# Gated delta-rule attention with a softplus feed-forward: the layout of the transposed inverses, and where the key norm is applied

## The chip, the cores and the metric

The kernel runs on one core of a Trainium2 chip, in one launch. The metric is device time in microseconds (us), median of the runs. A core has a matrix engine (PE in the profile; loading its stationary operand is listed apart, as PEld), a vector engine (DVE), an activation engine (ACT), a general engine (POOL) and a queue engine (SP) that here only starts DMAs. Each engine works through its own instruction stream in order; semaphores tie the streams together.

## The reference

```
k_n = k / (norm(k) + 1e-6)
for t in range(768):                      # for each of 4 batches x 8 heads
    readout = q[t] @ state                # state: 48 x 48
    y[t]    = g[t] * readout
    state  += beta[t] * outer(k_n[t], v[t] - state^T k_n[t])
x   = y laid out as (3072 tokens, 384)
out = softplus(x @ w_in) @ w_out          # 384 -> 2048 -> 384
```

All inputs and the output are float32; the kernel calculates in float16 with float32 accumulation.

## The kernel before

The recurrence is cut into 12 chunks of 64 steps. Inside a chunk it is solved in closed form: with the Gram matrix of the chunk's keys, a 64x64 unit triangular system per head has to be inverted. Each 64x64 inverse is built from 32x32 blocks, and each of these from 16x16 blocks. Between chunks only the state is passed on. The feed-forward ("dense") part of a chunk, or of a pair of chunks, can start once that chunk's y is there, and it fills the matrix engine while the recurrence of later chunks waits.

Work is described as items, each with the engines that may run it. One hand-laid string, `_ORDER`, lists all items with engine letters (D, A, G = POOL, P, S); it sets the order of every engine's stream, and buffers are given out in that order too.

The items by stage, with their lines:

- **front** (L262): the k and q of a chunk are cast to float16 ("cast", L200 on POOL or DVE, L198 on ACT), transposed on PE (L289), copied out ("kev"), and multiplied into the Gram matrices (L396, L397). The keys are raw here, not divided by their norm. "kkc" copies the negated key Gram blocks to `kk`; "mask" (L414) the masked query Gram blocks to `mt`.
- **norms** (L435), for a pair of chunks: square (ACT, L441), reduce (DVE, L445), root (on ACT at L456 for the first two pairs, else as a power of one half on POOL, L461), plus 1e-6 (L464). "lbeta" (L472) transposes the norms, takes the reciprocal, and multiplies it twice into beta: four short DVE instructions.
- **inverse** (L467), for a pair of chunks: "ln" (L481) transposes 32x32 blocks of `kk` on DVE; 15 substitution steps of two instructions each (L504, L511) invert the 16x16 diagonal blocks, on DVE for the first pair, on POOL for the other five; "c16" casts the result to `tw`. Then DVE transposes it back: "tn" once (L524) and "t32" twice (L534), in 32x32 blocks. Two PE products (xmm L555, tmm L576 and L582), with the copies "xs" and "td2" behind them, complete the 32x32 inverses in `td`; zmm (L608, L611) and its copy make `z`, the off-diagonal part.
- **chain** (L632), chunk after chunk: "vs" (L657) multiplies v by the norm, on POOL or DVE; ks and qs multiply with the state (L649); w = v - ks (L681); umm (L690, L694) applies the 32x32 inverses, zu (L715) the rest; smm and "s" update the state (L735, L750); ymm and "y" give the output (L765, L780); ytr transposes it (L797).
- **dense** (L812): g1 (L825), softplus on ACT (L837), g2 (L852), copy and store.

The layout that the change is about: `tn` is `[P, U, 16]` and `td` is `[P, U, HC]`, with U = 32 the blocks and HC = 32 the columns. A block's columns lie side by side for PE. The DVE transposes write them through a rearranged view:

```python
tn.ap.rearrange("p u j -> p j u")                        # L525: step of 16 elements
td.ap.rearrange("p u i -> p i u")[:, 16*b : 16*b + 16]   # L535: step of 32 elements
```

PE reads them as moving columns, `tn.ap[r, u, :]` and `td.ap[QUAD[qd], u, 16:]`, and in umm as the stationary operand, `td.ap[f, 16*cl + 2*pi + m, :]`.

Of the kernel before, what the change touches and what calls it, by code (L numbers as in the profile page):

```python
# [11 lines left out]
F16 = mybir.dt.float16  # L12
AF = mybir.ActivationFunctionType
ALU = mybir.AluOpType

# [59 lines left out]
def kernel(  # L75
# [11 lines left out]
    nc = tc.nc  # L87
# [54 lines left out]
    r_tn = ring("tn", 2, [P, U, 16], F16)  # L142
    r_xs = ring("xs", 2, [P, U, 16], F16)
    r_td = ring("td", 3, [P, U, HC], F16)
# [6 lines left out]
    r_ga = ring("ga", 18, [P, 512], F16)  # L151
# [33 lines left out]
    for t in r_t16.tiles:  # L185
        nc.vector.memset(t, 0.0)
    for t in r_kqt.tiles:
        nc.vector.memset(t[:, 4 * NP * C :], 0.0)
# [73 lines left out]
    def front(c, kk):  # L262
# [5 lines left out]
        for name, ring_ in (("k", r_kn), ("q", r_qn)):  # L268
# [3 lines left out]
            for h in range(parts):  # L272
                sl = slice(h, h + 1) if parts == 2 else slice(0, 2)
                x_it.append(
# [160 lines left out]
    def norms(cs, nv, on_act):  # L435
# [17 lines left out]
        tag = f"{cs[0]}"  # L453
        if on_act:
            root = add("sqrt", tag, "A",
                       lambda en: nc.scalar.activation(nv.ap, nv.ap, AF.Sqrt),  # L456
                       deps=red, bufs=[nv])
            root_last[0] = root
        else:
            root = add("pow", tag, "G",  # L460
                       lambda en: nc.gpsimd.tensor_tensor(nv.ap, nv.ap, half_c, ALU.pow),  # L461
                       deps=red, bufs=[nv])
        return add("eps", tag, "D",
                   lambda en: nc.vector.tensor_scalar_add(nv.ap, nv.ap, 1e-6),  # L464
                   deps=[root], bufs=[nv])

    def inverse(cc, kk, kk_it, nv, nv_it):  # L467
        tag = f"{2 * cc}"
        first = cc == 0
        nl, bl = Buf(r_nl), Buf(r_bl)  # L470

        def lbeta(en):  # L472
            nc.vector.transpose(nl.ap, nv.ap)
            nc.vector.reciprocal(nl.ap, nl.ap)
            nc.vector.tensor_tensor(bl.ap, beta_l[:, cc], nl.ap, ALU.mult)
            nc.vector.tensor_tensor(bl.ap, bl.ap, nl.ap, ALU.mult)

        bl_it = add("lbeta", tag, "D", lbeta, deps=[nv_it], bufs=[nv, nl, bl])
# [11 lines left out]
                       bl.ap.rearrange("p (b i) -> p b i", b=2),  # L490
                   ),
                   deps=[prev, bl_it], bufs=[tt, bl])

        def prep(en, b):
            r = slice(16 * b, 16 * b + 16)
            eng.tensor_tensor(  # L496
                nn.ap[:, b], ln.ap[:, r, r], bl.ap[:, r, None].broadcast_to([P, 16, 16]),
                ALU.mult,
            )
# [13 lines left out]
        for b in range(2):  # L513
            prev = add("prep", f"{tag}.{b}", en0, lambda en, b=b: prep(en, b),
                       deps=[l1, prev, bl_it], bufs=[ln, nn, bl])
        for j in range(15):
# [8 lines left out]
                        tn.ap.rearrange("p u j -> p j u"),  # L525
# [4 lines left out]
        for b in range(2):  # L530

            def t32(en, b=b):
                c0 = 16 - 16 * b
                nc.vector.transpose(  # L534
                    td.ap.rearrange("p u i -> p i u")[:, 16 * b : 16 * b + 16],  # L535
# [10 lines left out]
        halves = [[0], [1]] if first else [[0, 1]]  # L546
        td2 = {}
        e3s = []
        for cl in range(2):

            def xmm(en, cl=cl):
                for u in range(16 * cl, 16 * cl + 16):
                    for qd in range(4):
                        r = slice(32 * qd, 32 * qd + 16)
                        nc.tensor.matmul(  # L555
                            uv(xp.ap)[QUAD[qd], u], kk.ap[r, 0, u, :], tn.ap[r, u, :]
                        )

            e3s.append(add("xmm", f"{2 * cc + cl}", "P", xmm, deps=[tn_it], bufs=[kk, tn, xp],
# [9 lines left out]
        e5s = []  # L569
        for cl in range(2):  # L570

            def tmm(en, cl=cl):
                us = slice(16 * cl, 16 * cl + 16)
                for qd in range(4):
                    r = QUAD[qd]
                    nc.tensor.matmul(  # L576
                        uv(ep.ap)[r, us], ident[r, r], td.ap[r, us, 16:],
                        start=True, stop=False, skip_group_check=True,
                    )
                for u in range(16 * cl, 16 * cl + 16):  # L580
                    for qd in range(4):
                        nc.tensor.matmul(  # L582
                            uv(ep.ap)[32 * qd : 32 * qd + 16, u],
                            xs.ap[QUAD[qd], u, :],
                            td.ap[QUAD[qd], u, 16:],
# [5 lines left out]
            e5s.append(add("tmm", f"{2 * cc + cl}", "P", tmm, deps=[e4s[cl]] + td_its,  # L591
                           bufs=[xs, td, ep], mm=68, mode="3232"))
        for hs in halves:
            us = slice(16 * hs[0], 16 * hs[-1] + 16)
            it = add("td2", f"{2 * cc + hs[0]}", "AD",
                     lambda en, us=us: copy(en, td.ap[:, us, 16:], uv(ep.ap)[:, us]),
# [392 lines left out]
```

## Time and profile before

| | |
|---|---|
| runs | 308.46, 310.68, 305.07 us; median 308.46 |
| the profiled execution | 306.28 us |
| its span in the profile | 304.6 us |
| mean granted PE clock in the span | 0.943 |
| ACT busy | 131.4 us |
| POOL busy | 120.5 us |
| DMA moved | 27.69 MB in 107704 packets |
| code fetches on the instruction queue q8 | 47 packets, 0.77 MB |

The span is what the profile shows from the program's first instruction to its last; the execution's own time has another 1.7 us around it. An engine's busy time counts overlapping instructions once. The page's slices cut the span into 40 parts of 7.6 us; a digit is the busy tenths of a slice. A group line names the source line, engine, operation, the tiles written and read, the shapes and the count; behind the first bar are the busy time and the mean duration of one, behind the second the idle time of that engine just before them and what ended it. The view of waits lists who waited for whom, with the total, the number of times and the longest.

### The profile page before, as it was taken

The numbers are of one execution on the slowest core, as the hardware profiler recorded it, in microseconds if no ns is written. First come the engines' busy times: TensorE is split into PE (matmuls) and PEld (weight loads), VectorE is DVE, ScalarE is ACT, GpSimd is POOL, SyncE is SP. The second block draws the span as 40 slices with busy tenths as digits, with TensorE's granted clock in tenths as the row PEclk, the third lists the DMA queues.
The fourth block names the chain that finished last, engine by engine and source line by source line (L and its number), as shares of the span: only waits on it lengthen the run. The fifth ranks groups of instructions, "written<-read, shape, count | busy, mean of one in ns | idle before, by whom it ended". The sixth has DMA issues, their size and how long they took to land.

```text
span 304.6 us, 13469 instructions
## 1 busy us (share of the span) xinstructions
PE 241.7 (79%) x6112; PEld 160.8 (53%) x6112; DVE 184.7 (61%) x348; ACT 131.4 (43%) x250; POOL 120.5 (40%) x219
## 2 busy tenths in 40 slices
PE   1432347789959996869877999969899969999993
PEld 1232236568637763446643565635566635577771
DVE  7789936367696776974873467668486193432100
ACT  4541413347513666244423466613553425433441
POOL 7205335008892588458516203885007810000000
PEclk9999999999969999799985799995999988999999
DMA  9999999999900197983979521341035110002113
GB/s 126 152 140 151 171 143 181 185 168 142 130 2 4 31 163 130 156 132 55 167 109 146 109 56 30 62 68 30 4 83 106 27 28 18 14 22 63 26 26 78
DMA packets 107704, 27.69 MB, mean 91 GB/s; under 512 B 100864, under 2 KB 107648, under 8 KB 107648
## 3 DMA queue, kind: packets, MB, share of 16 engines
q1 hardware_dynamic: 101600, 23.21, 48.5%
q0 software_dynamic: 3968, 3.25, 6.7%
q8 instruction: 47, 0.77, 1.1%
q10 hardware_dynamic: 2080, 0.39, 0.9%
q14 instruction: 9, 0.07, 0.1%
HBM read 25.26 MB, written 4.72 MB: 98 GB/s over the span
## 4 chain that ended last, share of the span: by engine, by line
PE 46%; DVE 21%; POOL 17%; issue 10%; ACT 3%; DMA 2%; DVEq 0%; POOLq 0%; ACTq 0%
PE h L825 14%; PE o L852 14%; POOL tmp L504 8%; POOL tt L511 7%; DVE td L534 4%; DVE tn L524 3%; DVE ln L481 3%; PE d L649 3%; DMA kf<-in_k_dram 2%; PE d L715 2%; DVE tt L511 2%; PE d L289 2%; POOL nn L496 2%; DVE tmp L504 2%; PE d L765 1%
## 5 line engine op out<-in xcount | busy, mean ns | idle before, releaser
L825 PE MATMUL h<-xt,w_in 128*128 128x512 f16 (+1 forms) x384 | 82.0, 352 | 0.0
L852 PE MATMUL o<-w_out,ga 128*128 128x384 f16 x384 | 77.7, 345 | 2.3 <-issue 1.7
L837 ACT ACTIVATE ga<-h 128x512 f16<-128x512 f32 x96 | 56.3, 596 | 40.3 <-PE h L825 33.6
L852 PEld LDWEIGHTS <-ga 128*128 128x128 f16 x384 | 37.3, 102 | 28.9 <-issue 8.9
L825 PEld LDWEIGHTS <-w_in 128*128 128x128 f16 x384 | 36.5, 103 | 22.6 <-issue 5.3
L504 POOL TENSOR_TENSOR tmp<-nn,tt 128x30 f32<-128x30 f32 (+7 forms) x75 | 29.0, 387 | 5.9
L511 POOL TENSOR_TENSOR tt<-tt,tmp 128x30 f32<-128x30 f32 (+7 forms) x75 | 27.7, 369 | 5.9
L534 DVE STREAM_TRANSPOSE td<-tw 128x512 f16<-128x512 f16 x12 | 28.7, 2452 | 0.0
L461 POOL TENSOR_TENSOR nv<-nv,half_c 128x32 f32<-128x32 f32 x4 | 21.8, 5446 | 9.1 <-DVE nv L445 9.1
L200 DVE CAST u<-d 128x384 f16<-128x384 f32 x23 | 12.5, 552 | 19.4 <-PE d L715 15.3
L414 DVE TENSOR_TENSOR mt<-d,mask 128x256 f16<-128x256 f32 x40 | 16.8, 435 | 9.8 <-ACT kk L198 6.7
L198 ACT ACTIVATE u<-d 128x384 f16<-128x384 f32 x25 | 12.1, 492 | 23.4 <-PE d L715 12.7
L198 ACT ACTIVATE kqt<-d 128x512 f16<-128x512 f16 x26 | 15.1, 597 | 16.0 <-PE d L289 10.4
L555 PE MATMUL d<-tn,kk 16*32 16x16 f16 x768 | 7.3, 173 | 16.8 <-DVE tn L524 13.3
L289 PE MATMUL d<-ident,kn 128*128 128x128 f16 x96 | 9.1, 250 | 13.1 <-DVE kn L200 6.1
L198 ACT ACTIVATE osb<-o 128x384 f32<-128x384 f32 x14 | 6.9, 492 | 27.2 <-PE o L852 26.9
L496 POOL TENSOR_TENSOR nn<-ln,bl 128x256 f32<-128x256 f16 x10 | 6.3, 650 | 30.9 <-DVE ln L481 30.9
L649 PE MATMUL d<-s,kqt 48*64 48x48 f16 x704 | 16.7, 192 | 1.7 <-issue 1.4
L649 PEld LDWEIGHTS <-kqt 48*64 48x64 f16 x704 | 13.5, 112 | 8.4 <-issue 7.7
L555 PEld LDWEIGHTS <-kk 16*32 16x32 f16 x768 | 7.1, 93 | 18.8 <-issue 15.2
L657 POOL TENSOR_TENSOR vf<-vf,nv 128x768 f32<-128x768 f32 x8 | 11.8, 1472 | 13.2 <-DMA vf<-in_v_dram 13.2
L780 DVE TENSOR_TENSOR yg<-d,gf 128x384 f16<-128x384 f32 x24 | 12.8, 551 | 5.7 <-PE d L765 5.6
(100 smaller groups left out, 405.1 us busy)
## 6 DMA issues: line engine op xcount, KB each, us to landing
qf<-in_q_dram SPq DMA_DIRECT2D x24, 192.0 KB, 5.7
vf<-in_v_dram SPq DMA_DIRECT2D x24, 192.0 KB, 5.8
gf<-in_g_dram SPq DMA_DIRECT2D x24, 192.0 KB, 5.5
out_dram<-osb SPq DMA_DIRECT2D x48, 96.0 KB, 2.2
kf<-in_k_dram SPq DMA_DIRECT2D x22, 192.0 KB, 5.5
w_in<-in_moe_w_in_dram POOLq DMA_DIRECT2D x4, 384.0 KB, 6.6
w_out<-in_moe_w_out_dram POOLq DMA_DIRECT2D x4, 384.0 KB, 10.2
kf<-in_k_dram ACTq DMA_DIRECT2D x2, 192.0 KB, 4.5
```

Source lines behind the costliest of these rows:

```text
L198: nc.scalar.activation(o, x, AF.Copy, scale=float(sign))
L289: nc.tensor.transpose(o[:, p, i], x.ap[:, p, 2 * i : 2 * i + 2].rearrange("p h d -> p (h d)"), ident,)
L414: nc.vector.tensor_tensor(mt[c][m].ap[:, NP * p : NP * p + NP], gb[m].ap.rearrange("p (n b) -> p n b", n=NP)[:, :, C:], mask[:, None, :].b ...
L461: lambda en: nc.gpsimd.tensor_tensor(nv.ap, nv.ap, half_c, ALU.pow),
L504: eng.tensor_tensor(t, nn.ap[:, :, j + 1 :, j : j + 1].broadcast_to([P, 2, n, w]), tt.ap[:, :, j : j + 1, :w].broadcast_to([P, 2, n, w]), ...
L511: eng.tensor_tensor(rows, rows, t, ALU.add)
L534: nc.vector.transpose(td.ap.rearrange("p u i -> p i u")[:, 16 * b : 16 * b + 16], tw.ap[:, b, :, c0 : c0 + 32],)
L555: nc.tensor.matmul(uv(xp.ap)[QUAD[qd], u], kk.ap[r, 0, u, :], tn.ap[r, u, :])
L649: nc.tensor.matmul(hd(o.ap)[HALF[r], NP * p + i], kq_of(c, p)[FEAT[m], 2 * i + r, off : off + C], s0[r].ap[FEAT[m], NP * p + i], **start(p ...
L825: nc.tensor.matmul(hp.ap[:, n * b : n * b + n], w_in[:, j, f * P : (f + 1) * P], xt.ap[:, j, t0 : t0 + n], start=(j == 0), stop=(j == 2),)
L837: lambda en, hp=hp, o=gb: nc.scalar.activation(o.ap, hp.ap, AF.Softplus),
L852: nc.tensor.matmul(op.ap[:, :DM], b.ap[:, col + c0 : col + c0 + 128], w_out[:, f, :], start=(f == 0), stop=(f == NF - 1),)
```

## The change

1. `tn` becomes `[P, 16, U]` and `td` becomes `[P, HC, U]`: the order in which the DVE transposes produce their elements, so they write without a step. PE now reads a block's columns with a step of 32 elements (64 bytes): in xmm, tmm and zmm as moving operand, in umm as stationary operand. The identity products of tmm and zmm write PSUM with a step too; td2's copy has both sides without one. `td` gets four buffers in place of three; `ga` 17 in place of 18.
2. For all chunks from 2 on, the cast of k is replaced by a multiplication with the reciprocal norm ("unit"). With that the Gram blocks need no norm: "lbeta" and "vs" go for these chunks, and a reciprocal is added behind the 1e-6. The first pair stays as it was.
3. The root may run on ACT or POOL for pairs from chunk 4 on. In the new order the pair 4/5 has it on ACT, behind the Softplus table load.
4. At the start, `kk`'s first half (three buffers) and `nv` (three) are set by DVE.
5. The first pair's xs and td2 are no longer done in two halves.
6. `_ORDER` is written anew for all engines; the number of items goes from 1227 to 1210.

```diff
+GROUPS = [[c, c + 1] for c in range(0, 12, 2)]
...
-    r_tn = ring("tn", 2, [P, U, 16], F16)
+    r_tn = ring("tn", 2, [P, 16, U], F16)
...
-    r_td = ring("td", 3, [P, U, HC], F16)
+    r_td = ring("td", 4, [P, HC, U], F16)
...
-    r_ga = ring("ga", 18, [P, 512], F16)
+    r_ga = ring("ga", 17, [P, 512], F16)
...
+    for t in r_kk.tiles:
+        nc.vector.memset(t[:, 0], 0.0)
+    for t in r_nv.tiles:
+        nc.vector.memset(t, 1.0)
...
+                if name == "k" and nv is not None:
+
+                    def unit(en, f=f, x=x):
+                        ENG[en].tensor_tensor(
+                            x.ap[:, :, :, :D],
+                            f.ap,
+                            nv.ap[:, 16 * cl : 16 * cl + 16]
+                            .rearrange("p (a h) -> p a h", a=2)[:, :, :, None]
+                            .broadcast_to([P, 2, H, D]),
+                            ALU.mult,
+                        )
+
+                    x_it.append(
+                        add("unit", f"kn{c}.{h}", "GD", unit, deps=fl + [nv_it], bufs=[f, x, nv])
+                    )
+                    continue
...
+        def sqrt(en):
+            if en == "A":
+                nc.scalar.activation(nv.ap, nv.ap, AF.Sqrt)
+            else:
+                nc.gpsimd.tensor_tensor(nv.ap, nv.ap, half_c, ALU.pow)
+
+        root = add("sqrt", tag, "A" if on_act else "GA", sqrt, deps=red, bufs=[nv],
+                   size=0 if on_act else 1)
...
+        def eps(en):
+            nc.vector.tensor_scalar_add(nv.ap, nv.ap, 1e-6)
+            if inv:
+                nc.vector.reciprocal(nv.ap, nv.ap)
...
-                        tn.ap.rearrange("p u j -> p j u"),
+                        tn.ap,
...
-                    td.ap.rearrange("p u i -> p i u")[:, 16 * b : 16 * b + 16],
+                    td.ap[:, 16 * b : 16 * b + 16],
...
-        halves = [[0], [1]] if first else [[0, 1]]
+        halves = [[c % 2 for c in cs]]
...
-                            uv(xp.ap)[QUAD[qd], u], kk.ap[r, 0, u, :], tn.ap[r, u, :]
+                            uv(xp.ap)[QUAD[qd], u], kk.ap[r, 0, u, :], tn.ap[r, :, u]
...
-                        uv(ep.ap)[r, us], ident[r, r], td.ap[r, us, 16:],
+                        iu(ep.ap)[r, :, us], ident[r, r], td.ap[r, 16:, us],
...
-                            uv(ep.ap)[32 * qd : 32 * qd + 16, u],
+                            iu(ep.ap)[32 * qd : 32 * qd + 16, :, u],
                             xs.ap[QUAD[qd], u, :],
-                            td.ap[QUAD[qd], u, 16:],
+                            td.ap[QUAD[qd], 16:, u],
...
-                     lambda en, us=us: copy(en, td.ap[:, us, 16:], uv(ep.ap)[:, us]),
+                     lambda en, us=us: copy(en, td.ap[:, 16:, us], iu(ep.ap)[:, :, us]),
...
-                    nc.tensor.matmul(o[f], ident[f, f], td.ap[f, 16 * cl : 16 * cl + 16])
+                    nc.tensor.matmul(
+                        o[f].rearrange("p u i -> p i u"),
+                        ident[f, f],
+                        td.ap[f, :, 16 * cl : 16 * cl + 16],
+                    )
...
-                            td.ap[QUAD[2 * r + 1], 16 * cl + u, :],
+                            td.ap[QUAD[2 * r + 1], :, 16 * cl + u],
...
-        vs = add("vs", f"{c}", "GD",
+        vs = None if nv is None else add("vs", f"{c}", "GD",
...
-                            o[f, pi], td.ap[f, 16 * cl + 2 * pi + m, :], w1.ap[f, pi]
+                            o[f, pi], td.ap[f, :, 16 * cl + 2 * pi + m], w1.ap[f, pi]
...
-        nv_it = norms(cs, nv, cc < 2)
-        inverse(cc, kk, kk_it, nv, nv_it)
+        inv = cs[0] > 1
+        kk_it = []
+        nv_it = norms(cs, nv, cs[0] < 4, inv)
+        for c in cs:
+            kk_it += front(c, kk, nv if inv else None, nv_it)
+        inverse(cs, kk, kk_it, nv, nv_it, inv)
...
 _ORDER = """
-S8 A9 D126 D154 P129 D130 A1 A125 P127 A148 D149 P140 S0 G104 D142 A128 P137 D139 A146 A141 D147
...
+S8 A9 D131 P133 S0 A1 S11 S16 S2 S10 A132 A106 P135 S17 A136 D107 D134 S3 G111 A104 D154 G110 P114
...
```

In the new order POOL has all ten unit multiplications. Its stream around the first of them, with item names in place of numbers, runs: two parts of w_in, vs of chunk 1, unit of chunk 2, the other two parts of w_in, unit of chunk 3, the four parts of w_out, then the first POOL inverse; behind that inverse unit 5, unit 4, the root of pair 6, unit 6, unit 7, and the inverse of pair 4.

## The prediction

> **What bounds the kernel now.** I read the busy table and the slices first, then the chain of work that ended last, then the waits, then the groups of the transposes, then the chain in order of time around one stall.
>
> ```profile
> PE 241.7 (79%) x6112; PEld 160.8 (53%) x6112; DVE 184.7 (61%) x348; ACT 131.4 (43%) x250; POOL 120.5 (40%) x219
> PE   1432347789959996869877999969899969999993
> DVE  7789936367696776974873467668486193432100
> PEclk9999999999969999799985799995999988999999
> DMA  9999999999900197983979521341035110002113
> PE 46%; DVE 21%; POOL 17%; issue 10%; ACT 3%; DMA 2%; DVEq 0%; POOLq 0%; ACTq 0%
> ```
>
> PE is the engine to relieve: from slice 8 (about 61 us) on it is full except in a few dips. At the dips of slices 11, 16, 20, 27 and 32 DVE is busy, and the granted clock falls too. Ahead of 60 us PE is mostly idle, waiting for the first two chunks while DMA is full.
>
> ```profile
> PE d L555 <- DVE tn L524: 13.3, 5, 3.6
> PE d L576 <- DVE td L534: 2.5, 2, 2.2
> PE d L715 <- issue: 4.5, 2, 2.3
> L534 DVE STREAM_TRANSPOSE td<-tw 128x512 f16<-128x512 f16 x12 | 28.7, 2452 | 0.0
> L524 DVE STREAM_TRANSPOSE tn<-tw 128x512 f16<-128x512 f16 x6 | 14.3, 2377 | 2.6 <-POOL tw L200 2.4
> L481 DVE STREAM_TRANSPOSE ln<-kk 128x1024 f16<-128x1024 f16 x6 | 11.4, 1907 | 2.2 <-ACT kk L198 2.0
> ```
>
> The first row of waits is the largest that PE has: five of the six inverses end with PE standing for tn. The transposes explain it: ln moves 1024 elements per partition in 1907 ns, tn and td only 512 in 2377 and 2452. ln reads with a step and writes without; td reads without and writes with one. So the stepped write costs most of a td, and tn, which has both, is no slower.
>
> ```profile
> 83.98 0.47 DVE tw L200
> 84.48 2.37 DVE tn L524
> 86.89 1.19 PE d L555 x114
> 88.08 4.93 PE o L852 x16
> ...
> 263.88 2.60 PE o L852 x16
> ```
>
> One inverse ends: cast, tn, then xmm; PE stood 3.55 us (from 83.34). The 16 dense products after it take 4.93 us, at 264 us the same 16 take 2.60: the throttle granted half the clock. So a stall is paid twice.
>
> **The change part by part.** Sums are against the profiled execution, 306.28 us (span 304.6 and 1.7 around it); the median is 308.46, 2.2 higher, the three runs lie between 305.07 and 310.68.
>
> *Transposes on DVE.* No contiguous 16-bit transpose of this size is in the trace. Nearest: DVE copies from PSUM, 256 elements in 415 ns (L202) and 512 in 690 (z, L200): 1.07 ns an element and 141 fixed, so td comes to 141 + 512 x 1.07 = 690 ns. tn keeps a stepped read; by ln, 1907/1024 = 1.86 ns an element, 950 ns. Ends for td: no gain (2450), if the transpose itself is slow, which ln's 1.86 against 4.8 speaks against; 690 as the good end. I take 690: 12 x 1.76 = 21 us and 6 x 1.43 = 8.6 us less on DVE. Most lies beside PE's work. On the path: at the start tn and both t32 stand in line (tn from 27.5, second t32 ends 35.20): 1.43 + 2 x 1.7 = 4.9 us. In the five later groups tn's 1.43 each: 7.2. The PE wait for td in the pair 6/7: 2.2. Total 14.3. What is late next: c16, the PE-ACT-PE steps through xs and td2, and code fetches, which the rows call issue.
>
> *Clock.* The granted clock is 0.943 of the span: 304.6 x 0.057 = 17 us lost to the half clock, of which PE works some 15 (the half-speed stretches hold few idle us). Here the trace and a page of the Trainium skill differ. The stretches start shortly behind PE stalls of 3.55, 2.54, 2.19, 2.82 and 2.90 us (at 83, 120, 156, 203 and 245 us). The Trainium skill, "TensorE: Matmul & The Clock Gate", section "HAM oscillation — how this bites in real kernels", gives the rule as no idle gap above about 3.4 us. By the rule only the first stall would trip it, and shortening the others would bring nothing: 3.4 us (half of one stretch of about 7). By the trace gaps under 3 us do it too, beside the tiny xmm products, and shortening all could return 15. I take the middle, 7: gaps between 1 and 1.5 us remain, and whether they trip it no row shows.
>
> *The stepped read on PE.* This speaks against the change. Columns with a step, per chunk, in series on one quarter of the array: xmm 16 x 16 = 256; tmm 256 in the identity product and 16 x 16 = 256; zmm 512 and 16 x 32 = 512; umm 2 x 8 x 32 = 512 stationary. Together 2304, times 12 chunks = 27,650. A column costs PE now 2.60 us/(16 x 384) = 0.42 ns. No PE row reads with a step. Lower end: nothing extra (a gain is excluded[...]). Nearest row: DVE's stepped read, 1.86 ns against 1.07 contiguous, a factor 1.74. As a factor it gives 0.31 ns more a column, 8.6 us. As an absolute price of memory, 1.86 - 0.42 = 1.44 ns more, 39.8 us. The Trainium skill, "Advanced Engine Details and Errata", sections "SBUF Cachelines" and "PSUM Cachelines", is against the change in both places: one access per 16-byte line is penalised, and "Any non-contiguous AP significantly slows down matmuls" in PSUM, which hits the 1024 columns per chunk that tmm and the identity product of zmm write. It has no figure. By it alone I would lean to the upper end and forecast no gain; by the row read as a factor, a gain stays. I take 8.6 and keep 0 and 40. If xmm's 64 products, about 0.62 us now, are bound by issue and weight loads, part of it is hidden.
>
> *Keys divided when cast.* Ten multiplications on POOL (nearest: vs, L657, 1.47 us): +14.7. Away on POOL: six vs (8.8), five k casts at 0.83 (4.1), one power of 5.45 (L461). On DVE: four vs (0.95), one k cast (0.64), five lbeta of 0.94 less five reciprocals of 0.35: 7.4 less. ACT loses four k casts (3.4). Busy time of all three falls, but the norm now stands ahead of transposes and Gram. Queued behind a unit on POOL: for the first two, half of w_in and all w_out DMAs. vs of chunk 1 waited to 43.3 for v; then unit 2, two w_in parts, unit 3, w_out: the weights are issued at about 46 to 53, as against 30 to 53 before. The first g1 (52 us) uses the two early parts; the others land some 7 us later, ahead of their g1 after 65. I take 0, with 3 us if that cover is gone. For the pair 4/5: units behind the POOL inverse, then the power of pair 6 (5.45), a q cast (0.85) and two units (2.9) before the next inverse: 12 us, against 20 between these inverses before (84 to 104). PE needs about 15 us for trs, Gram and the chain in between, so ln is later than POOL: 0 again, up to 3 a group if not. On SP the k loads of both chunks must have landed, and stores stand among loads as before; the count of DMAs is unchanged.
>
> *Root on ACT for the pair 4/5.* Softplus is loaded by then, so two more table loads (L158 and L884: 1283 ns each). ACT is 43% busy; one lies where ACT waits for PE between xs and u1. I take 1.3 of 2.6 us, ends 0 and 2.6.
>
> *Start.* DVE's memsets run without idle to 5.65, where the first k cast starts at once. Three memsets of 1024 float16 (tt has the same 2048 bytes, 0.49 us at L486) and three small ones of 0.1 add about 1.7 us. k0 lands only at 9.0 and DVE has 1.4 us of gaps until then; 1.0 stays. The joined halves of xs and td2 in the first pair cost one longer copy, 0.6 against 0.39 (L198, xs), on the path twice: 0.4. The extra td buffer lets inverses run ahead, one ga less binds softplus sooner: both 0.
>
> Sum: -14.3 - 7 + 8.6 + 1.3 + 1.0 + 0.4 = -10; 306.3 - 10 = 296.3. The rest of DVE's relief (some 20 us that is not on the path now) shortens the queues in front of w, u and s; no row prices it, and the new order may spend or add to it. I forecast 296.
>
> **The rivals.**
> *Stepped columns at the full price (slower).* PE is the bound from 61 us on, so 39.8 in place of 8.6 goes straight to the end: 296.3 + 31 = 327. For it: PE is 79% busy and the skill's rule; against it: the four row groups read side by side and loads overlap. The point of decision: the gains less the small costs are 18.6 us, so 18.6/27,650 = 0.67 ns extra a column is no change, 0.90 is 2% slower. 20%, spread over 308 to 328.
> *Reads cost nothing and the throttle never trips.* 0 in place of 8.6, 15 in place of 7: 280. For it: 9 to 10 ns per small product is more than 16 columns need. 22%.
> *The stalls only change their name.* PE waits for keys that wait for norms, or for code: L715's issue waits of 2.3 us fall at fetches of code while DMA is full, which nothing here removes. The 7.2 and 7 are lost: 310 at most, 306 likely. 16%.
> *The transposes don't get faster.* Then only costs stay, 318; ln makes that unlikely. 2%.
>
> **How the numbers follow.** The likeliest, 40%: 296, on its own 289 to 304 (clock 3 to 15, issue cover). Range: 279 takes in most of the second case, 318 half of the slower one; about 10% lies above and 8% below. A measurement of this kernel tells about 2% from no change (302.3 to 314.6). Faster: 0.36 of the likeliest, 0.22, and 0.02 of the third: 0.60. Within 2%: 0.04 + 0.13 + 0.03 = 0.20. Slower: 0.17 + 0.01 + 0.02 = 0.20.
>
> **What would show it.** td near 0.7 us and tn near 0.95 in the DVE groups; PE's wait for tn at 6 us or less in place of 13.3; a mean clock over 0.96; xmm, tmm and zmm busy times (7.3, 8.1, 8.2 us; 5.5 for zmm's identity) up by less than a half. Wrong would be: zmm's identity product at twice its 455 ns or more, a unit multiplication among PE's releasers for over 5 us, or ga waiting for the second table load.

## The result, and the profile after

| | before | after |
|---|---|---|
| median of four runs | 307.22 us (305.07 to 310.68) | 283.77 us (282.21 to 285.31) |
| ratio | | 0.9258 (0.9155 to 0.9362) |
| the profiled execution, its span | 306.28, 304.6 us | 282.21, 280.3 us |
| mean granted PE clock in the span | 0.943 | 0.994 |

The kernel is 7.4% faster. Direction and range held; the gain, 23 us between the medians, is about twice the forecast's 10 to 12. Some executions of a kernel take over 1.5% longer than its fastest: medians are of all executions, ratios (with their 95% interval) leave those out. The page of after, busy table, slices (now 7.0 us each) and the shares of the chain that ended last:

```profile
PE 238.7 (85%) x6112; PEld 165.1 (59%) x6112; DVE 153.7 (55%) x333; ACT 130.2 (46%) x248; POOL 114.1 (41%) x217
...
PE   0540579979978998899998999999999999999993
...
DVE  7899645482266787856684585561764242413000
...
PEclk9999999999979999999999999999999999999999
DMA  8999968999972399921885980510233410110123
...
PE 50%; POOL 21%; DVE 13%; issue 13%; ACT 2%; POOLq 0%; DVEq 0%
```

PE is full from slice 6 (42 us) on, where before it was full from slice 8 (61 us). DVE's share of the chain fell from 21% to 13%, that of "issue" rose from 10 to 13. The row of the granted clock dips once, before five times. The transposes did what was asked of them, and PE paid for it (view of groups, shapes kept apart, after):

```profile
L741 PE MATMUL d<-w,td 32*32 32x48 f16 x384 | 13.8, 214 | 0.4 <-ACT td L205 0.4
L658 PE MATMUL d<-td,kk 32*32 32x32 f16 x384 | 13.2, 227 | 0.0
L741 PEld LDWEIGHTS <-td 32*32 32x32 f16 x384 | 12.1, 144 | 0.9 <-ACT td L205 0.8
...
L564 DVE STREAM_TRANSPOSE tn<-tw 128x512 f16<-128x512 f16 x6 | 8.7, 1454 | 11.3 <-POOL tw L207 9.1 <-ACT tw L205 2.2
...
L625 PE MATMUL d<-td,xs 32*16 32x16 f16 x768 | 8.4, 185 | 5.2 <-issue 5.2
L651 PE MATMUL d<-td,ident 32*32 32x512 f16 x24 | 8.1, 670 | 0.0
...
L574 DVE STREAM_TRANSPOSE td<-tw 128x512 f16<-128x512 f16 x12 | 8.0, 688 | 0.0
```

A td fell from 2452 to 688 ns, a tn from 2377 to 1454. Before, the products of umm (L694, with the load of td as its weights) and of zmm (L611, and L608 for the identity product) stood at:

```profile
L694 PE MATMUL d<-w,td 32*32 32x48 f16 x384 | 8.8, 187 | 2.8 <-issue 2.8
L694 PEld LDWEIGHTS <-td 32*32 32x32 f16 x384 | 6.6, 94 | 3.1 <-issue 3.1
L611 PE MATMUL d<-td,kk 32*32 32x32 f16 x384 | 8.2, 176 | 2.2 <-issue 2.2
L608 PE MATMUL d<-td,ident 32*32 32x512 f16 x24 | 5.5, 455 | 0.0
```

Where the 24 us went is read best from PE's windows. The last product ends at 300.4 us before and at 275.9 after; the first product of g1 starts at 52.2 and at 45.0. The rows are start:end, length, then the busy time of PE, PEld, DVE, ACT and POOL, the granted clock, the DMA share and GB/s; first before, then after:

```profile
52.20:300.40 248.20, 221.54 (x5364) 144.70 (x5362) 145.22 (x248) 112.15 (x213) 100.66 (x185) 0.93 0.47 78
```

```profile
45.00:275.90 230.90, 219.90 (x5382) 149.69 (x5378) 119.79 (x235) 110.62 (x211) 98.15 (x187) 0.99 0.53 91
```

Three differences make up the 24.5 us: the first g1 starts 7.2 us sooner; behind it PE is idle for 230.9 - 219.9 = 11.0 us in place of 26.7, so 15.7 less; its work takes 1.6 less. In the last, two large terms nearly cancel: the stepped operands (14 us more, below), and less time at half clock. By the clock's own records that is 34.1 us against 3.4 behind the first g1. But the records begin only at 68.7 us before and at 56.0 after, and ahead of them the row reads full speed where PE had half: six products of g1 take 1.46 us at 52.2, 61.8 and 66.3 us before and at 45.0 and 51.9 after, and 0.83 from 55.9 on. So the half-clock time behind the first g1 is nearer 50 and 14 us, and the mean clocks of the first table are too high, the one of before more so.

The 7.2 us at the start are mostly waits of PE for its own instructions ("issue"). Both kernels begin umm at the same time; what follows up to the first g1 (chain in order of time, before):

```profile
37.06 0.07 PE d L694 x3
37.12 2.96 issue
...
43.18 2.28 issue
...
50.26 1.39 issue
...
52.23 1.40 PE h L825 x6
```

The same stretch, after, in which no such wait is longer than 0.04:

```profile
37.13 0.47 PE d L741 x10
...
45.06 1.40 PE h L872 x6
```

Before, these three waits take 6.6 of 15.2 us; after, the stretch takes 7.9. The view of waits, after:

```profile
PE d L598 <- DVE tn L564: 10.4, 5, 7.0
...
PE d L625 <- issue: 5.2, 3, 3.8
```

PE still stands 10.4 us for tn, but 7.0 of them are at the start, once. In the five later pairs it is 3.4. Before, the same row read 13.3, of which 3.3 lay at the start: 10.0 in the later pairs.

### The profile page after: what moved, and what is told of

It reads as the page before. It is cut to its first block, busy times and chain, and to the rows that moved or that the text cites. A ratio compares the mean times of both kernels' runs of the same rounds, so it can differ in the third digit from the quotient of the medians.

```text
span 280.3 us, 13451 instructions
## 1 busy us (share of the span) xinstructions
PE 238.7 (85%) x6112; PEld 165.1 (59%) x6112; DVE 153.7 (55%) x333; ACT 130.2 (46%) x248; POOL 114.1 (41%) x217
## 4 chain that ended last, share of the span: by engine, by line
PE 50%; POOL 21%; DVE 13%; issue 13%; ACT 2%; POOLq 0%; DVEq 0%
PE h L872 15%; PE o L899 13%; POOL tt L551 8%; POOL tmp L544 8%; PE d L696 3%; DVE ln L521 3%; PE d L658 2%; POOL kn L284 2%; PE d L312 2%; PE d L741 2%; PE d L625 2%; PE d L812 2%; PE d L762 2%; DVE tmp L544 2%; POOL nn L536 2%
## 5 line engine op out<-in xcount | busy, mean ns | idle before, releaser
L872 PE MATMUL h<-xt,w_in 128*128 128x512 f16 (+1 forms) x384 | 75.3, 331 | 1.9 <-ACT ga L884 1.9
L899 PE MATMUL o<-w_out,ga 128*128 128x384 f16 x384 | 73.3, 332 | 0.6 <-ACT osb L205 0.6
L899 PEld LDWEIGHTS <-ga 128*128 128x128 f16 x384 | 35.6, 99 | 24.0 <-issue 2.4
L544 POOL TENSOR_TENSOR tmp<-nn,tt 128x30 f32<-128x30 f32 (+7 forms) x75 | 26.9, 359 | 5.8
L207 DVE CAST u<-d 128x384 f16<-128x384 f32 x21 | 11.5, 555 | 22.7 <-PE d L741 9.0
L536 POOL TENSOR_TENSOR nn<-ln,beta_l 128x256 f32<-128x256 f16 x10 | 6.3, 650 | 40.4 <-DVE ln L521 40.2
L481 POOL TENSOR_TENSOR nv<-nv,half_c 128x32 f32<-128x32 f32 x3 | 16.5, 5504 | 12.8 <-DVE nv L468 12.8
L207 DVE COPY osb<-o 128x384 f32<-128x384 f32 x12 | 6.6, 548 | 27.4 <-PE o L899 27.4
L205 ACT ACTIVATE kqt<-d 128x512 f16<-128x512 f16 x26 | 15.2, 595 | 13.8 <-DVE kqt L207 10.4
L205 ACT ACTIVATE u<-d 128x384 f16<-128x384 f32 x27 | 12.9, 489 | 17.6 <-PE d L741 10.2
L284 POOL TENSOR_TENSOR kn<-kf,nv 128x768 f16<-128x768 f32 x10 | 14.7, 1475 | 14.3 <-DVE nv L491 10.6
L827 DVE TENSOR_TENSOR yg<-d,gf 128x384 f16<-128x384 f32 x24 | 12.9, 553 | 8.5 <-PE d L812 7.5
L312 PE MATMUL d<-ident,kn 128*128 128x128 f16 x96 | 9.1, 250 | 8.7 <-DVE kn L207 7.6
L598 PE MATMUL d<-tn,kk 16*32 16x16 f16 x768 | 7.3, 184 | 10.6 <-DVE tn L564 10.4
L696 PEld LDWEIGHTS <-kqt 48*64 48x64 f16 x704 | 12.7, 112 | 5.8 <-issue 4.6
L205 ACT ACTIVATE kk<-d 128x256 f16<-128x256 f32 x33 | 11.3, 384 | 8.3 <-DVE mt L437 4.1
L564 DVE STREAM_TRANSPOSE tn<-tw 128x512 f16<-128x512 f16 x6 | 8.7, 1454 | 11.3 <-POOL tw L207 9.1
```

Of the source, the lines that this page charges most:

```text
L205: nc.scalar.activation(o, x, AF.Copy, scale=float(sign))
L207: ENG[en].tensor_copy(o, x)
L284: ENG[en].tensor_tensor(x.ap[:, :, :, :D], f.ap, nv.ap[:, 16 * cl : 16 * cl + 16] .rearrange("p (a h) -> p a h", a=2)[:, :, :, None] .broa ...
L312: nc.tensor.transpose(o[:, p, i], x.ap[:, p, 2 * i : 2 * i + 2].rearrange("p h d -> p (h d)"), ident,)
L544: eng.tensor_tensor(t, nn.ap[:, :, j + 1 :, j : j + 1].broadcast_to([P, 2, n, w]), tt.ap[:, :, j : j + 1, :w].broadcast_to([P, 2, n, w]), ...
L696: nc.tensor.matmul(hd(o.ap)[HALF[r], NP * p + i], kq_of(c, p)[FEAT[m], 2 * i + r, off : off + C], s0[r].ap[FEAT[m], NP * p + i], **start(p ...
```

## The experiments

In the expectations, S is the theory that the layout brings most of the gain, through shorter stalls; O that the new order with the keys brings the larger part; K that the place of the key norm is worth much by itself, R that the sequence of work is what counts; F that the early stalls of PE for its own code come from the weight DMAs beside them; N that the sequence does it, above all the early place of two pieces of PE work at the start. "Before" stands for a run of the kernel before on the same chip.

**The two halves apart.** One kernel has the layout alone, with the old order and keys; the other has order and keys, in the old layout. Layout alone, in the kernel before:

```diff
-    r_tn = ring("tn", 2, [P, U, 16], F16)
+    r_tn = ring("tn", 2, [P, 16, U], F16)
-    r_td = ring("td", 3, [P, U, HC], F16)
+    r_td = ring("td", 3, [P, HC, U], F16)
...
-                            uv(xp.ap)[QUAD[qd], u], kk.ap[r, 0, u, :], tn.ap[r, u, :]
+                            uv(xp.ap)[QUAD[qd], u], kk.ap[r, 0, u, :], tn.ap[r, :, u]
```

> The kernel before with the new layout of tn and td alone: old order, keys as before, td three buffers. Theory S (short transposes end both the stalls and the throttling, whatever the order): at least two thirds of the 23 us, so 292 us or less, and a mean granted clock of 0.98 or more. Theory O (the layout alone is worth what its terms gave in the forecast, the new order does the rest): 296 to 300 us, clock 0.95 to 0.97.

Order and keys alone is the same edit backwards, in the kernel after:

```diff
-    r_td = ring("td", 4, [P, HC, U], F16)
+    r_td = ring("td", 4, [P, U, HC], F16)
...
-                    td.ap[:, 16 * b : 16 * b + 16],
+                    td.ap.rearrange("p u i -> p i u")[:, 16 * b : 16 * b + 16],
```

> The changed kernel with tn and td put back in the old layout (stepped write on DVE, contiguous columns for PE), everything else as changed. Theory S: the stalls and the half clock come back, 300 us or more, clock 0.95 or less. Theory O: 294 us or less, since the order carries the gain; the products that read with a step get cheaper by about 13 us of PE busy time.

Layout alone: 299.52 us (294.24 to 304.27), before 306.09. Order and keys alone: 291.53 us, ratio 0.9542 (0.9408 to 0.9676). As the first spread widely, both it and the kernel after were run again, together:

> The layout alone in the old order, as the upper end on this chip: 299, with a ratio of 0.97 to 0.985.

> The changed kernel itself, as the lower end on this chip: 284, with a ratio of 0.92 to 0.935.

300.05 us, ratio 0.9684 (0.9578 to 0.9789), and 285.14 us, ratio 0.9265 (0.9195 to 0.9334). So by the medians the layout is worth 6.6 to 6.7 us in the old order, and 6 to 8 in the new (291.5 against 285.1 and 283.8), and order and keys about 15 in either. The ratios give the layout more, near 10 us in the old order (6.5 to 12.9) and 8 to 9 in the new, and order and keys 13 to 14. By both, the two add up and order and keys are the larger part. O held; S, with its 292 us or less, fell. And the layout alone left the start where it was (view of waits, layout alone):

```profile
PE d L558 <- DVE tn L524: 9.2, 4, 3.4
...
PE d L585 <- issue: 5.5, 2, 3.2
PE d L701 <- issue: 4.4, 1, 4.4
```

Its first g1 starts at 51.7 us (51.9 in the second run), against 52.2. In front of it PE now stood 4.4 us and 3.2 us for its own instructions ("issue"), right behind the shortened transposes.

**Which part of order and keys.** First the keys: the new order and layout, but every key raw again, with the norm in beta and in a multiplication of v ("vs").

```diff
-    r_nv = ring("nv", 3, [P, 32], F32)
+    r_nv = ring("nv", 6, [P, 32], F32)
...
-                        add("unit", f"kn{c}.{h}", "GD", unit, deps=fl + [nv_it], bufs=[f, x, nv])
+                        add("unit", f"kn{c}.{h}", "GD", unit, deps=fl, bufs=[f, x])
...
-            nv_of[c] = (None if inv else nv, nv_it)
+            nv_of[c] = (nv, nv_it)
```

> The changed kernel (new layout, new order) with the keys of later chunks treated as before: a plain cast in the place of the unit multiplication, the four short lbeta instructions behind the norm, and v multiplied by the norm, for eight of these ten chunks on POOL and for two on DVE, just ahead of where w needs it. Theory K (dividing the keys at the cast gives a good part of the 15 us that layout does not explain): 290 us or more. Theory R (the sequence of work gives it, and the keys are worth what POOL and DVE save off the path, near nothing): within 2% of the changed kernel, 281 to 288 us.

299.42 us, ratio 0.9786 (0.9705 to 0.9867): some 15 us lost, more than the keys can be worth, as the second form shows. The view of waits shows why:

```profile
PE d L749 <- DVE w L740: 7.1, 1, 7.1
```

One multiplication of v had been laid on POOL behind a whole inverse; w, and PE with it, waited. The second form puts two of these multiplications on DVE instead:

```diff
-... S58 D279 G343 G1211 S59 D652 ...
+... S58 D279 G343 S59 D1211 D652 ...
-... G394 G1212 P956 D334 D671 ...
+... G394 P956 D334 D1212 D671 ...
```

> As old_keys, but with v of chunks 3, 4, 5 and 6 multiplied on DVE directly ahead of w, and the other six on POOL; in old_keys one multiplication stood behind an inverse on POOL and PE waited 7.1 us for it. Theory K (the place of the norm matters by itself): still 290 us or more. Theory R (what old_keys lost was that one place): 288 us or less.

291.69 us, ratio 0.9385 (0.9296 to 0.9473). Against the kernel after (0.9258 and 0.9265) the keys are worth about 1.2% or 4 us; the intervals overlap, so the size is rough. By its time K's mark of 290 us is met, by its ratio (288 us beside 307) R's of 288: the place of the norm counts, but is the smaller part.

Then the order, in one place. The new order runs the query Gram of chunk 1 (gramq) with its two masks, and half the query transposes of chunk 2 (trs), ahead of the first inverse's end, where PE waits for tn. This kernel puts them where the old order has them, behind chunk 0's ymm and smm. (The old order has transposes of chunk 2's keys in front of xmm; this kernel has nothing in their stead, since with unit keys they come later.) In the items' names:

```diff
-P gramq 1, D mask, D mask, P trs q2.0, A kev
 P xmm 0
...
 P ymm 0, P smm 0
+P gramq 1, P ytr 0, P trs q2.0, A kev, D mask, D mask
 P g1 0
```

> The changed kernel with two pieces of PE work put back to their old place: the query Gram of chunk 1 with its two masks behind the first state update, and the query transpose of chunk 2 behind the first output transpose (in the changed order both run while PE waits for the first inverse). Theory N (the early gain comes from filling PE's waits at the start): the first dense product at 47 us or later in place of 45, and 1.5 us or more lost in all. If the start does not carry through: 284 us within 1%.

290.31 us, ratio 0.9404 (0.9356 to 0.9452), 4 to 5 us lost. The chain in order of time up to the first g1 (start, length, engine, line), first with the two pieces late, then after:

```profile
37.59 2.13 issue
...
40.77 0.61 ACT z L205
...
44.34 0.44 PE d L382 x28
...
46.52 0.87 PE d L312 x8
47.41 0.03 ACT kqt L205
47.44 0.57 issue
48.01 1.28 ACT L933
49.30 0.20 ACT dummy L933
...
50.67 1.40 PE h L872 x6
```

```profile
32.32 3.80 issue
...
36.48 0.61 ACT td L205
...
38.73 0.61 ACT z L205
...
45.06 1.40 PE h L872 x6
```

g1 starts 5.6 us later. Of these only 1.3 are the two pieces' own work (0.44 and 0.87, L382 and L312). 2.1 are a wait of PE for its instructions in front of zmm, which the kernel after does not have there, and 1.5 are the load of the softplus table with its first call (L933): ACT now took it up behind the late copy of the queries (47.41) and z of the second chunk waited for it, while in the kernel after it runs at 41.3 us with nobody waiting. N held here. A piece of work moved off the path takes with it what gathers around it.

Both parts undone together in one kernel (raw keys and the late place), and, in another, the early place given to the layout alone in the old order. The second one's edit, in the items' names:

```diff
+P gramq 1, D mask, D mask, P trs q2.0, A kev
 P xmm 0
...
 P smm 0
-P gramq 1, D mask, D mask, P trs q2.0, A kev
```

> The changed kernel with both taken out: the two pieces of PE work back in their late place and the keys treated as before (the multiplications of v placed as in old_keys2). If these two are all that order and keys give: within 1% of lay_only on this chip, about 299. If the rest of the order has a share of its own: 295 or less.

> The kernel before with the new layout, and in the old order the query Gram of chunk 1 with its masks, the mask of chunk 0 and the query transpose of chunk 2 moved ahead, to where the changed order has them; nothing else. Theory N (filling PE's waits at the start is worth 5 to 6 us wherever it is done): first dense product at 48 us or earlier, in place of 52, and at least 3 us less than lay_only on this chip. Else: within 1 us of lay_only; then the early gain needs more of the new order.

Keys raw and the two pieces late: 297.88 us, ratio 0.9679 (0.9605 to 0.9754), the same as the layout alone in the old order (0.9684). So these two account for all that order and keys bring; the rest of the new sequence is worth nothing that shows (the intervals leave room for some 3 us). The early place in the old order: 301.61 us (295.65 to 304.77), no gain over 300.05 (295.65 to 304.70). There the early gramq (L359) stood for a mask that DVE had not done yet (view of waits, early place in the old order):

```profile
PE d L359 <- DVE mt L370: 6.2, 1, 6.2
```

So N holds as far as it says that the gain is lost without the early place, and falls where it says that the place suffices: what the pieces need must be early too.

| kernel | first g1 at, us | PE idle behind it, us | last product, us | median, us |
|---|---|---|---|---|
| before | 52.2 | 26.7 | 300.4 | 307.22 |
| layout alone, second run | 51.9 | 17.6 | 295.0 | 300.05 |
| order and keys alone | 44.3 | 20.4 | 283.5 | 291.53 |
| both parts undone (late, raw keys) | 52.1 | 14.2 | 291.8 | 297.88 |
| two pieces late | 50.6 | 11.5 | 283.7 | 290.31 |
| raw keys, second form | 45.1 | 15.3 | 285.6 | 291.69 |
| after | 45.0 | 11.0 | 275.9 | 283.77 |

(Idle is the window from the first g1 to the last product, less PE's busy time in it. One profiled execution each, so a us or two of it is chance.)

**The weights' transfers.** Before, three parts of w_in are issued ahead of v's multiplication for chunk 1; here two of these are put behind it, and in the kernel after, where two are ahead, the other two are put ahead as well (first pair of lines: before; second: after).

```diff
-... P584 G97 G96 P579 ... D144 G98 S15 ... S43 G99 A195 ...
+... P584 G97 P579 ... D144 S15 ... S43 G99 G96 G98 A195 ...
...
-... A590 P874 G98 G591 ... G231 G97 P595 ... D217 G99 G211 ...
+... A590 P874 G98 G97 G99 G591 ... G231 P595 ... D217 G211 ...
```

> The kernel before with two of the three early w_in parts (1.6 MB) issued behind v's multiplication for chunk 1, at about 45 us in place of 30, as in the changed order; nothing else moved. Theory F (early on PE stands for its own code, because the weights fill the DMA queues just then): PE's issue stalls of 2.8, 2.3 and 1.4 us between 37 and 52 us get shorter, the first dense product starts at 48 us or earlier in place of 52, and the time falls by 3 to 6 us. Theory N (the sequence on PE and DVE does it): first dense product at 51 to 52 us, time unchanged within 1%.

> The changed kernel with the two late parts of w_in issued at about 26 us, together with the first two, in place of 44 us. Theory F: code stalls appear between 36 and 50 us, the first dense product starts at 48 us or later in place of 45, 287 us or more. Theory N: first dense product at 45 us, time within 1% of 284.

308.28 us (303.29 to 309.17; before 307.24, 303.71 to 308.90): the first g1 came at 50.5 in place of 52.2, two of the three waits above were shorter (1.4 and 1.7 us in place of 2.8 and 2.3), and no gain shows at the end. With two issued early in the kernel after: 286.82 us, ratio 0.9344 (0.9248 to 0.9439): g1 still at 44.6; some 1% lost, and the intervals overlap. F fell: its marks were 48 us and a gain of 3 to 6.

The traces do show what these waits follow. The longer ones end about 1.5 us behind the landing of a 16 KB packet on the instruction queue q8: before, packets land at 32.4, 38.6, 43.9 and 50.0 us, and PE goes on at 33.9, 40.1, 45.5 and 51.7. And in every one of the profiled executions the first g1 goes with one packet: where the view of transfers has one on q8 between 20 and 30 us, while PE stands for tn anyway, the first g1 comes at 43.9 to 46.0 us (after, order and keys alone, both forms with raw keys, and all others with the new order); where it has none, at 50.5 to 52.7 (before and its variants in the old order, layout alone, two pieces late, both undone, and the early place in the old order, where gramq stood for its mask). Between 28 us and the first g1 PE stands for its instructions for nothing of note in order and keys alone, 3.8 us after, 5.6 and 5.8 with the two pieces late, 7.7 before and 9.3 to 9.5 in the layout alone. So the two pieces, run ahead of the wait for tn, most likely bring the fetch of the next stretch of PE's code into that wait. No run moves code and nothing else: this is read from the traces, not shown by an experiment.

**The price on PE.** The identity product of zmm can step in PSUM, where it writes (as after), or in its read:

```diff
-                        o[f].rearrange("p u i -> p i u"),
+                        o[f],
                         ident[f, f],
-                        td.ap[f, :, 16 * cl : 16 * cl + 16],
+                        td.ap[f, :, 16 * cl : 16 * cl + 16].rearrange("p i u -> p u i"),
```

> The changed kernel with the identity product of zmm turned round: it reads td with a step of 64 bytes and writes PSUM without one, in place of reading runs of 16 elements and writing PSUM with a step of 128 bytes. If the step in PSUM is what takes this product from 455 to 670 ns: it falls to 480 or less and the time to about 281. If a stepped read costs as much: 650 or more and the time stays at 284 within 1%.

287.43 us, ratio 0.9444 (0.9375 to 0.9513), 2 to 6 us more than with the step in PSUM. The same product in order and keys alone (contiguous on both sides), then with the stepped read:

```profile
L651 PE MATMUL d<-td,ident 32*32 32x512 f16 x24 | 5.2, 427 | 0.0
```

```profile
L651 PE MATMUL d<-td,ident 32*32 32x512 f16 x24 | 12.7, 1042 | 0.0
```

For 512 columns a read in steps of 64 bytes costs (1042 - 427)/512 = 1.2 ns a column, a PSUM write in steps of 128 bytes (670 - 427)/512 = 0.47 (its read then goes in runs of 16 elements, which cost nothing in tmm's identity product, below).

The next kernel removes the stepped reads of zmm and umm, and with them the new memsets. The product of tmm, 512 columns wide here, turns the block order in PSUM, and the copy behind it stores contiguous blocks, `tu`:

```diff
-    r_td = ring("td", 4, [P, HC, U], F16)
+    r_td = ring("td", 1, [P, HC, U], F16)
+    r_tu = ring("tu", 3, [P, U, HC], F16)
...
-                            td.ap[QUAD[2 * r + 1], :, 16 * cl + u],
+                            tu.ap[QUAD[2 * r + 1], 16 * cl + u, :],
```

> A version without the startup memsets in which PE reads no td column with a step: tmm's identity product takes all 32 rows and writes PSUM block by block (a step in PSUM), td2 copies both halves out in block order to a second tile, and zmm and umm read that tile contiguously. Costs: 24 identity products at about 670 ns in place of 294, four side by side, and one more copy of 0.6 us for each of the six pairs. By the measured terms zmm, umm and zmm's identity product give back some 14 us of PE busy time and tmm takes 4 to 5: if PE is the bound, 276 to 281 us; if the longer way through td2 stands in the chain, 284 or more.

```profile
L619 PE MATMUL d<-td,ident 32*32 32x512 f16 x48 | 8.2, 667 | 0.2 <-DVE mt L390 0.2
...
L742 PE MATMUL d<-w,tu 32*32 32x48 f16 x384 | 7.9, 183 | 0.0
L659 PE MATMUL d<-tu,kk 32*32 32x32 f16 x384 | 7.6, 174 | 0.0
...
L656 PE MATMUL d<-tu,ident 32*32 32x512 f16 x24 | 5.1, 419 | 0.5 <-ACT tu L202 0.5
```

The products are back at their old durations. The time is 285.16 us, ratio 0.9224 (0.9168 to 0.9281), beside 0.9258 for the change: no difference that shows. By the expectation PE's bound would have given 276 to 281. In the profiled execution PE is idle for 13.9 us behind the first g1 (after 11.0) and busy for 221.3 (after 219.9); it runs at half clock for 26.6 us there, after for some 14, which may be what ate the products' gain. That is not shown: in its four runs the mean clock lay between 0.938 and 0.982, and the one at 0.982 was the slowest (286.05).

**Clock and memsets.** In the kernel before, twelve idle 128x512 products (their result is overwritten) in front of xmm fill PE's wait for tn in the five later pairs:

```diff
+                if cl == warm[cc] and not first:
+                    for _ in range(12):
+                        nc.tensor.matmul(xp.ap, w_in[:, 0, :P], w_in[:, 0, :512])
```

> The kernel before with 12 idle products of 128x512 (about 2.6 us at full clock) on PE just ahead of the first xmm of each of the five later pairs, where PE waits for tn 1.0 to 3.6 us anyway; they write a buffer that xmm overwrites. If the throttle is a cost of its own: the granted clock rises from 0.943 to 0.97 or more and the time falls by 5 to 12 us, to 295 to 302, although every transpose is as slow as before. If the half clock only accompanies work that is late anyway: no change or up to 5 us slower (307 to 312).

309.93 us, ratio 1.0103 (1.0039 to 1.0167). Half clock behind the first g1 fell from 34.1 to 20.5 us by the records (from about 50, counting what lies ahead of them); the time did not fall. It doesn't settle the clock's own worth: the 60 products took PE 13.8 us of busy time, of which the window's idle time gave only 4.3 (26.7 to 22.4).

The memsets of `kk` and `nv` removed from the kernel after, four lines of the change:

```diff
-    for t in r_kk.tiles:
-        nc.vector.memset(t[:, 0], 0.0)
-    for t in r_nv.tiles:
-        nc.vector.memset(t, 1.0)
```

> The changed kernel without the six memsets that it adds at the start on DVE (the buffers are written in full before they are read). If they hold up the first key cast as forecast: first transpose on PE at 6.1 us in place of 7.6, and 0.5 to 1.5 us less in all, 282 to 283. If the later loads set the start: no change, 284.

283.56 us, ratio 0.9281 (0.9199 to 0.9364): nothing.

## Why the prediction was half right

The whole came out at -10 to -12 us by the forecast and at -22 to -24 by the runs. The error is in one step, with a smaller one of the other sign beside it. That the time fell within the range is in part luck: two wrong terms of opposite sign.

**The step that failed: order and keys at nothing.** The text took "I take 0" for the keys and said of the new order that "no row prices it, and the new order may spend or add to it". With memsets, table loads and joined halves, the forecast for all that is not layout was +2.7 us. The runs showed -13 to -15, with the old layout or the new: some 4 from unit keys, 4 to 5 from the early place of gramq and trs, the rest only with both (with both undone the gain is gone whole). At the start it came through PE's waits for its own instructions, 6.6 us between umm and the first g1, which the forecast named but gave no price in its sum. The early place could have been found: before, PE stood idle ahead of xmm (3.3 us at 26.6) and ran gramq and trs behind smm, between chunk 0's chain and the first g1; the two order strings could have been laid over that stretch. What the forecast did instead was to price the start by DVE's transposes alone.

**The layout, a term too good.** Forecast for it: -14.3 - 7 + 8.6 = -12.7. Measured: -7 by the medians, near -10 by the ratio, whose interval just reaches the forecast.
- *td 690 ns*: 688. *tn 950 ns*: 1454, or 2.84 ns an element; its read steps by 96 bytes, ln's by 64 at 1.86. To take ln's price for tn was wrong.
- *Start, 4.9 us*: 0.3 to 0.5. What was late next were PE's own instructions, 4.4 and 3.2 us of "issue" in the layout alone. The prediction named code fetches as next, and gave them no price; the rival "the stalls only change their name" was right of this stretch.
- *Later groups, 7.2 + 2.2*: PE idle behind the first g1 fell from 26.7 to 17.6 to 19.5 us in the layout alone (its two runs), 7 to 9 us. Right in size. Its working counted five later pairs at tn; the row of five waits included the first pair (3.3 us), and at 205.6 us PE stood for mt (2.8), not tn.
- *Stepped reads, +8.6*: the products of zmm, umm and the zmm identity took 5.6, 5.7 and 2.9 us more busy time than in order and keys alone, 14. Mis-sized by 5.6 in total, for two mistakes that partly cancel. The columns were over-counted: the reads and writes of tmm's identity product run over 16 neighbours and cost nothing (294 ns, in order and keys alone 331), and the products of xmm and tmm with 16 columns next to nothing (184 and 185 ns against 171 and 169; busy time 7.3 and 8.4 us against 7.3 and 8.1), as the forecast had allowed for xmm. A third of the columns (768 of 2304 a chunk) thus paid next to nothing; the other 18,432 cost 14.2 us, 0.77 ns each and not 0.31. Here the Trainium skill, "Advanced Engine Details and Errata", section "SBUF Cachelines" (one access per 16-byte line is penalised), agrees in direction: the one long stepped read that was measured cost 1.2 ns a column, near the forecast's absolute reading of the DVE row (1.44) and not its reading as a factor. For PSUM, where the same page's section "PSUM Cachelines" calls any non-contiguous access a significant slowdown, a write in steps of 128 bytes cost 0.47 ns a column in zmm's identity product and nothing visible in tmm's products of 16 columns.
- *Clock, 7 us*: unsettled as a term. The recorded clock was 0.973 to 0.994 in the change's four runs, and half-clock time in the profiled one fell by some 36 us. But the forecast's price, 3 us for a point of mean clock, does not show between executions: in 34 runs of the kernel before the clock lay between 0.921 and 0.953, and time rose by 0.4 us a point (correlation 0.17); over all 104 runs, each beside the mean of its kernel, it fell by 0.8 (-0.36). These means are a weak measure, since they count the half-speed start as full (above). In the two profiles of the layout alone the half-clock time behind the first g1, start included, is 17 and 40 us, and the times are 294.24 and 300.96. The one recorded stretch in the kernel after ahead of the last product starts at 79.9 us, 0.8 us behind the end of a PE gap of 1.5 us: one case that suggests that gaps between 1 and 1.5 us can trip the throttle, which the forecast left open.

**What held.** PE as the bound; units on POOL are covered: no unit is among the releasers of PE's waits; the second table load did not hold ga back (PE waits for ga: 1.9 us in total, each at most 0.7); memsets were worth nothing, the forecast had +1.0. Of the marks set down, td near 0.7 and a clock over 0.96 came true, tn near 0.95 and "PE's wait for tn at 6 us or less" did not (10.4), the latter since the new order moved 7.0 of that wait to a place where it costs nothing extra: work that used to stand behind it was done already. zmm's identity stayed below twice 455 ns; zmm's products rose by 61% in busy time, over the half that was set as the limit.

**The rivals.** The full price of the stepped read (327) failed because a third of the columns paid next to nothing and the others half of it. "Reads cost nothing and the throttle never trips" (280) was near the time for a wrong reason: reads cost 14 us, and the new order paid for them. "The stalls only change their name" was right of the start and wrong behind it. "The transposes don't get faster" fell with td at 688 ns.

**What stays open.** Whether PE's waits for its instructions shrink because a code packet comes during the wait for tn, as the traces suggest (the weights' DMAs were tried and are not what sets them); the keys' exact share; what a point of clock is worth alone; why the block copy's 14 us did not reach the end.

## What to carry to other kernels

When a change comes with a new order of work, the order is a part with a price of its own: lay the two orders of the bound engine side by side over its idle stretches, and see which pieces move from behind a wait into it. Price what gathers around a moved piece as well (a table load, a code fetch, a mask). A stall's length before is no measure of the gain from shortening it; what stands second in line at that place is.

## What the hardware showed beyond expectation

- A 16-bit DVE transpose of 128x512 takes 688 ns with a contiguous write and a read in runs of 64 bytes, 1454 with a read in steps of 96 bytes and a contiguous write, 2452 with that read in runs and a write in steps of 64 bytes: here the step was dearer on the side of the write.
- On PE a stationary operand read in steps of 64 bytes costs 144 ns for 32 columns in place of 92 to 94, 1.6 ns a column; a product of 16 moving columns shows next to nothing of its step (173 and 184 ns), one of 32 goes from 175 to 227 ns, one of 512 from 427 to 1042.
- PE stood up to 4.7 us at a time for its own instructions in the first 40 us ("issue"), at places that moved with the order of the work more than with the weights' transfers. The longer waits end about 1.5 us behind the landing of a 16 KB packet on the instruction queue.
- The row of the granted clock reads full speed ahead of its first record (68.7 us before, 56.0 after), where six products of 256 columns take 1.46 us in place of 0.83.
